# Block attention inside a matmul pipeline: scores of both float32 parts in two full-height passes instead of three half-height pairs

## The chip, the cores and the metric

One core of a Trainium2 chip runs the whole program. The metric is the device time of one execution in microseconds (us), as the median of several executions.

## The reference

Three layers follow each other. The attention layer has 4 batches, 8 heads, 768 tokens and 64 elements per head; each token sees the 4 first keys (the sinks) and the 127 keys before it and itself (the window):

```python
scores = scale * np.matmul(q, k.transpose(0, 1, 3, 2))
keep = is_sink | in_window
scores = np.where(keep, scores, -1000000000.0)
scores = scores - np.max(scores, axis=-1, keepdims=True)
a = np.exp(scores)
a = a / (np.sum(a, axis=-1, keepdims=True) + 1e-09)
out = np.matmul(a, v)
```

Its output, 3072 tokens of 512 elements, goes through a layer of 512 x 2048 x 512 with a squared ReLU (`w_in`, `w_out`), and then through a layer of 8 experts, of which each token uses the one with its highest gate score (`w1`, `w2`).

## The kernel before, in words

The tokens are worked in 12 blocks of 256, numbered t = 0 to 11. The matmul layer of block t runs on TensorE while the attention of block t + 1 is woven between its pieces. A block of the matmul layer has 16 steps j: `l1` (L610) does 12 matmuls of 256 columns into the tile psh, `l2` (L635) does 6 matmuls of 512 columns into the pair psx. The last stage, the experts, comes after all attention.

Float32 values are held as two parts of 'fp32r' type, hi and lo, of which hi is a rounded copy and lo the rest. A product is made of three matmuls, hi times hi, hi times lo and lo times hi, from block 2 on (T32 = 2; the first two blocks use plain float32).

The attention of a block handles four pairs p of heads and, for each, two halves n of 128 queries. The two heads e = 0, 1 of a pair lie on rows 0 to 63 and 64 to 127. Its pieces are:

- `prep_k` (L366): three (or two) 128x128 transposes of keys into a tile psk_ of the one bank psT; ScalarE copies it to the hi part of kT (L387), VectorE subtracts to get the lo part (L388).
- `prep_q` (L395): two transposes of queries into a tile of the bank s0 (L400); hi by ScalarE (L415), lo by VectorE (L416). GpSimd then splits the values V (L422, L423).
- `scores` (L446): per head one bank, s0 for head 0 and s1 for head 1 (psS, one buffer each). Three rounds m, in each a matmul for head 0 and one for head 1, each with 64 rows of contraction:

```python
for m, (a_, b_) in enumerate(((0, 0), (0, 1), (1, 0)) if t >= T32 else ()):
    for e in range(2):
        r = slice(64 * e, 64 * e + 64)
        PE.matmul(ps[e][:, 0:W], lhsT=qt[r, a_, n, :], rhs=kt[r, b_, c0:c0 + W], start=(m == 0), stop=(m == 2))
```

  W is 260 columns (4 of them the sinks), 128 for the first 128 queries of a batch. Then VectorE takes mask and row maximum of each head (L469), ScalarE the exponential (L472), and sums, reciprocals and scaling follow (L474 to L484). GpSimd collects sink weights in psk (L487 to L489).
- `ptrans` (L492): the probabilities are transposed into the bank psT (L501), split by ScalarE and VectorE (L512, L513) and masked by GpSimd (L517).
- `pv` (L523): matmuls with V into pso (L543), which ScalarE, VectorE and GpSimd add up (L548 to L553).
- `fin_sink` (L557) transposes psk into the bank psT, `add_sink` (L565) adds the share of the sinks.

Each piece is an event with a place h on a scale of two per step j (`attn_events`, L585); `run_to` emits the events up to a place between `l1` and `l2`. LEADS (L36) says how many units before its scores a key and a query preparation stand, and how many after them the transposes and the pv step. The instructions so emitted are ordered by a list scheduler by priority, within what data and buffers allow; `tc.high_priority` raises that of what is emitted inside it. Each engine then works its list in order.

Of the kernel before, what the change touches and what calls it, by code (L numbers as in the profile page):

```python
# [29 lines left out]
HOME = 224  # L30
REG = NT + 128
XW = 513
T32 = 2


LEADS = ((5, 2, 4.5, 8.5), (5, 2, 4.5, 8), (5.5, 2.5, 4.5, 8))  # L36

SPLITS = {6: (0, 0), 8: (2, 0), 11: (0, 1), 12: (1, 0), 13: (2, 1), 14: (3, 0)}

# [7 lines left out]
def kern(ctx, tc, q, k, v, n_sink, window, w_in, w_out, w_gate, w_og, w1, w2, out):  # L47
# [282 lines left out]


    nat = {}
    qTt = {}
    kTt = {}
    Vt = {}
# [30 lines left out]
    def prep_k(t, p):  # L366
        o = 1 if t % 3 == 0 else 0
        x = nat.pop(("k", t, p))
        ps = psT.tile([128, 4, 128], F32, tag="T", name="psk_")
        if t == 0:  # L370
            fill(ps[:].rearrange("p n c -> p (n c)"), 1)
        for n in range(o, 3):
            PE.transpose(ps[:, n], x[:, n].rearrange("p h d -> p (h d)"), ident[:])
        kt = att.tile([128, 2, KS * 3], F32R, tag="kT", name="kT", bufs=2)
        kv = kt[:].rearrange("p a (n c) -> p a n c", c=KS)
        if t < T32:
            kf = kv[:, 0].bitcast(F32)
# [9 lines left out]
        A.activation(out=kv[:, 0, o:3, 0:128], in_=ps[:, o:3], func=AF.Copy)  # L387
        V.tensor_tensor(out=kv[:, 1, o:3, 0:128], in0=ps[:, o:3], in1=kv[:, 0, o:3, 0:128].bitcast(F32), op=ALU.subtract)  # L388
        if o:
            G.tensor_copy(out=sk[:, p], in_=kv[:, :, 1, 0:NS].bitcast(F32))  # L390
        for n in range(o, 2):
            G.tensor_copy(out=kv[:, :, n, 128:KS], in_=sk[:, p].bitcast(F32))
        kTt[t, p] = kt

    def prep_q(t, p):  # L395
        x = nat.pop(("q", t, p))
        if t < T32:
            ps = psO.tile([128, 4, 128], F32, tag="O", name="psq")
        else:
            ps = psS.tile([128, 260], F32, tag="s0", name="psq")[:, 0:256].rearrange("p (n c) -> p n c", n=2)  # L400
# [4 lines left out]
        o = att.tile([128, 2, 2, 128], F32R, tag="qT", name="qT", bufs=2)  # L405
        qTt[t, p] = o
        if t < T32:
            if p % 2:
                A.activation(out=o[:, 0].bitcast(F32), in_=ps[:, 0:2], func=AF.Copy)
            else:  # L410
                V.tensor_copy(out=o[:, 0].bitcast(F32), in_=ps[:, 0:2])
            Vt[t, p] = nat.pop(("v", t, p))
            more(t, p)
            return
        A.activation(out=o[:, 0], in_=ps[:, 0:2], func=AF.Copy)  # L415
        V.tensor_tensor(out=o[:, 1], in0=ps[:, 0:2], in1=o[:, 0].bitcast(F32), op=ALU.subtract)  # L416

        n0 = 1 if t % 3 == 0 else 0
        x = nat.pop(("v", t, p))
# [26 lines left out]
    def scores(t, p, n):  # L446
# [6 lines left out]
        if t == 0 and n % 2:  # L453
            ps = [psX.tile([128, 512], F32, tag=f"x{e}", name=f"psx{e}") for e in range(2)]
        else:
            ps = [psS.tile([128, 260], F32, tag=f"s{e}", name=f"pss{e}") for e in range(2)]
        if t == 0:
            fill(ps[0][:, 0:W], 2)
        for e in range(2 if t < T32 else 0):
            r = slice(64 * e, 64 * e + 64)  # L460
            PE.matmul(ps[e][:, 0:W], lhsT=qt[r, 0, n, :].bitcast(F32), rhs=kt[r, 0, c0:c0 + W].bitcast(F32), start=True, stop=True)
# [93 lines left out]
    skT = {}  # L555

    def fin_sink(t):  # L557
        ps = psT.tile([128, 4, 128], F32, tag="T", name="psst")
# [26 lines left out]
    def attn_events(t):  # L585

        ev = []
        h0 = 32 * (t - 1) - 8
        a0, a1, a2, a3 = LEADS[min(t, 2)]
# [601 lines left out]
```

## Time and profile before

| what | value |
|---|---|
| median of 3 runs | 1150.24 us (1148.74 to 1150.37) |
| the profiled execution | 1149.1 us, its span 1147.4 us |
| PE busy | 1120.3 us (98%) |
| VectorE (DVE) busy | 728.4 us (63%) |
| ScalarE (ACT) busy | 638.2 us (56%) |
| GpSimd (POOL) busy | 419.8 us (37%) |

The span runs from the first to the last instruction; the execution's own time is 1.7 us longer. Shares of busy time are means over stages: attention of blocks 3 to 11 stands between about 178 and 720 us, the experts behind about 760 us. A matmul's time in the profile is that from its entry to its modelled end, and matmuls overlap; so what one costs is read from the starts of those that follow.

### The profile page before, as it was taken

What the parts mean: (1) busy time and instruction counts of PE and PEld (TensorE: products, weight loads), DVE (VectorE), ACT (ScalarE), POOL (GpSimd) and SP (SyncE); (2) the same over time, 40 slices, a digit from 0 to 9 for tenths busy, and PEclk for the clock granted to TensorE, in tenths of its full rate; (3) what the DMA queues carried; (4) which work ended last, traced back from release to release, by engine and by line L of the source; (5) the groups of instructions that cost most, each with busy time, mean ns of one, the idle gap of its engine ahead of it and who ended that gap; (6) DMA issues with size and microseconds to landing.
All of it is one profiled execution on the core that took longest, in us unless ns stands there. A gap on an engine that the chain in (4) does not pass through costs nothing. (4 is left out here: it accounts for less than half of the span.)

```text
span 1147.4 us, 23733 instructions
## 1 busy us (share of the span) xinstructions
PE 1120.3 (98%) x7002; PEld 939.0 (82%) x7002; DVE 728.4 (63%) x2027; ACT 638.2 (56%) x1749; POOL 419.8 (37%) x917
## 2 busy tenths in 40 slices
PE   7999999999999999999999999999999999999995
PEld 4556788888888888888888888997788888888884
DVE  4899876676767667676667677567312576764153
ACT  4898676777677767676767777464232232232200
POOL 3112553355664336565326665210211112221111
PEclk8999999999999999999999999999999999999998
DMA  6677111111211111211112110295411456653110
GB/s 150 172 238 208 44 25 50 40 50 38 54 29 50 38 45 38 56 29 43 36 38 56 38 31 2 42 242 159 129 39 47 156 185 216 225 203 133 48 45 24
DMA packets 139391, 100.08 MB, mean 87 GB/s; under 512 B 103907, under 2 KB 112227, under 8 KB 139238
## 3 DMA queue, kind: packets, MB, share of 16 engines
q1 hardware_dynamic: 131476, 82.28, 25.6%
q0 software_dynamic: 5472, 14.19, 3.7%
q10 hardware_dynamic: 2290, 1.84, 0.5%
q8 instruction: 64, 1.05, 0.4%
q14 instruction: 89, 0.73, 0.2%
HBM read 85.56 MB, written 13.76 MB: 87 GB/s over the span
## 5 line engine op out<-in xcount | busy, mean ns | idle before, releaser
L619 PE MATMUL psh<-xT,WI 128*128 128x256 f32 x2112 | 280.2, 282 | 0.0
L619 PEld LDWEIGHTS psh<-xT,WI 128*128 128x128 f32 x2112 | 266.5, 188 | 9.7 <-issue 0.5
L956 PE MATMUL psh<-WI,xt 128*128 (+1 forms) x672 | 163.7, 398 | 1.1 <-ACT xt L936 0.7
L629 DVE TENSOR_TENSOR r<-r 128x256 f32<-128x256 f32 x180 | 83.4, 464 | 113.2 <-ACT r L622 113.1
L644 PE MATMUL psx<-WOb,h 128*128 128x512 f32 x576 | 153.9, 404 | 0.8 <-ACT h L631 0.4
L956 PEld LDWEIGHTS psh<-WI,xt 128*128 128x128 f32 x672 | 125.0, 190 | 27.3 <-ACT xt L936 0.9
L644 PE MATMUL psx<-WOa,h 128*128 128x512 f32 x528 | 144.7, 409 | 0.0
L644 PEld LDWEIGHTS psx<-WOb,h 128*128 128x128 f32 x576 | 101.7, 188 | 20.0 <-ACT h L631 1.4
L472 ACT ACTIVATE P<-P,st 128x260 f32<-128x260 f32 (+1 forms) x192 | 93.7, 488 | 43.5 <-DVE st L469 43.1
L972 DVE TENSOR_TENSOR ht<-psht,ht 128x512 fp32r<-128x512 f32 x56 | 38.5, 689 | 120.8 <-ACT ht L936 120.4
L622 ACT ACTIVATE r<-psh 128x256 f32<-128x256 f32 x192 | 71.7, 373 | 63.0 <-PE psh L619 59.1
L644 PEld LDWEIGHTS psx<-WOa,h 128*128 128x128 f32 x528 | 93.4, 190 | 15.6
L517 POOL TENSOR_SCALAR_AFFINE_SELECT PT<-PT 128x256 fp32r<-128x256 f32 x224 | 98.5, 473 | 16.1 <-DVE PT L513 15.9
L994 POOL DMA_INDIRECT out_dram<-xg,pidx x28 | 28.7, 1025 | 199.9 <-ACT xg L993 159.2
L632 DVE TENSOR_TENSOR h<-r,h 128x256 fp32r<-128x256 f32 x184 | 83.7, 455 | 18.0 <-ACT h L631 12.2
L631 ACT ACTIVATE h<-r 128x256 fp32r<-128x256 f32 x184 | 76.1, 414 | 28.6 <-DVE r L629 23.8
L469 DVE CUSTOM_DVE_ANT_0 P<-pss,M 128x260 f32<-128x260 f32 (+1 forms) x184 | 72.6, 403 | 23.0 <-PE pss L465 11.1
L962 ACT ACTIVATE r<-psh 128x512 f32<-128x512 f32 x48 | 28.8, 599 | 100.2 <-PE psh L956 98.4
L985 PE MATMUL psy<-WOb,ht 128*128 (+1 forms) x336 | 84.0, 398 | 0.0
L985 PE MATMUL psy<-WOa,ht 128*128 (+1 forms) x336 | 82.2, 391 | 0.0
L484 ACT ACTIVATE P<-P,st 128x132 f32<-128x132 f32 (+2 forms) x168 | 62.2, 415 | 34.4 <-DVE st L475 34.3
L553 POOL TENSOR_TENSOR xr<-tB,tC 128x128 f32<-128x128 f32 x80 | 38.4, 480 | 101.8 <-DVE tB L552 96.7
(450 smaller groups left out, 1963.1 us busy)
## 6 DMA issues: line engine op xcount, KB each, us to landing
raw<-in_moe_w_dram SPq DMA_DIRECT2D x36, 1024.0 KB
craw<-in_moe_w_out_dram SPq DMA_DIRECT2D x15, 512.0 KB
craw<-in_moe_w_in_dram SPq DMA_DIRECT2D x14, 512.0 KB
x2tab<-x2s SPq DMA_DIRECT2D x24, 256.5 KB
kn<-in_k_dram SPq DMA_DIRECT2D x64, 96.0 KB
vn<-in_v_dram SPq DMA_DIRECT2D x64, 96.0 KB
qn<-in_q_dram SPq DMA_DIRECT2D x92, 64.0 KB
kn<-in_k_dram SPq DMA_DIRECT2D x32, 64.0 KB
```

The costliest lines, as they stand in the source:

```text
L469: V.tensor_tensor_reduce(out=P[:, e, 0:W], in0=ps[e][:, 0:W], in1=mask[:, 0:W], scale=-SCALE, scalar=3.0e38, op0=ALU.add, op1=ALU.min, acc ...
L472: A.activation(out=P[:, e, 0:W], in_=P[:, e, 0:W], func=AF.Exp, scale=-1.0, bias=st[:, e:e + 1], accum_out=st[:, 4 + e:5 + e])
L484: A.activation(out=P[:, e, 0:W], in_=P[:, e, 0:W], func=AF.Copy, scale=st[:, 6 + e:7 + e])
L517: G.affine_select(out=both[:, 1 - b, e], in_=bf[:, 0, e], pattern=[[0, 2], [1 - 2 * b, 128]], compare_op=ALU.is_gt if b else ALU.is_ge, fi ...
L619: PE.matmul(ps[:], lhsT=WI[:, j, a_, kk, :], rhs=x[:, b_, kk, :], start=(n == 0), stop=(n == 11))
L622: A.activation(out=hq[:], in_=ps[:], func=AF.Relu)
L629: E_.tensor_tensor(out=hq[:], in0=hq[:], in1=hq[:], op=ALU.mult)
L631: A.activation(out=o[:, 0], in_=hq[:], func=AF.Copy)
L632: V.tensor_tensor(out=o[:, 1], in0=hq[:], in1=o[:, 0].bitcast(F32), op=ALU.subtract)
L644: PE.matmul(acc[t][m][:], lhsT=o[:, a_, 128 * m:128 * m + 128], rhs=WO[j // 8][:, j % 8, b_, :], start=(j == 0 and n == 0), stop=(j == NF ...
L956: PE.matmul(ps[:], lhsT=o[:, a_, kk, :], rhs=wview(n, par + 2048 * b_ + 512 * kk, 512), start=(c == 0), stop=(c == 11))
L985: PE.matmul(yp[s][:], lhsT=o[:, a_, kk, :], rhs=wview(2 + n, par + 2048 * b_ + 512 * kk, 512), start=(n == 0 and kk == 0 and c == 0), stop ...
```

## The change

From block 3 on (STK = 3), five things change:

- `scores` does two matmuls per head with 128 rows of contraction. The keys of head e lie as 128 rows in kT[:, e]: the hi part on the head's own 64 rows, the lo part on the other 64. The first matmul has the queries' hi part on both halves, the second the lo part on the head's own rows and zeros on the others. The sum is the same three products.
- `prep_k` writes its transposes to the bank s0, and ScalarE and VectorE each take two instructions of 64 rows instead of one of 128.
- `prep_q` keeps one tile qst for all later blocks; ScalarE and VectorE take two instructions of 64 rows each, and GpSimd copies the hi parts to the other half. The zeros are written once.
- The row maxima of both heads are emitted at a priority raised by 100; a line of LEADS for t = 3 and later moves keys (5.5 to 6.5 units ahead), transposes (4.5 to 3.95 units behind) and pv (8 to 7.92).
- `fin_sink` uses the bank s1 and stands 0.91 units later.

The buffer of the query tile goes from two of half the size to one of the same total size; blocks 0 to 2 compute as before.

```diff
+T32, STK = 2, 3
+HALF = (slice(0, 64), slice(64, 128))
-LEADS = ((5, 2, 4.5, 8.5), (5, 2, 4.5, 8), (5.5, 2.5, 4.5, 8))
+LEADS = ((5, 2, 4.5, 8.5), (5, 2, 4.5, 8), (5.5, 2.5, 4.5, 8), (6.5, 2.5, 3.95, 7.92))
...
     def prep_k(t, p):
-        ps = psT.tile([128, 4, 128], F32, tag="T", name="psk_")
+        if t < STK:
+            ps = psT.tile([128, 4, 128], F32, tag="T", name="psk_")
+        else:
+            ps = psS.tile([128, 512], F32, tag="s0", name="psk_")[:].rearrange("p (n c) -> p n c", n=4)
...
+        else:
+            for e in range(2):
+                A.activation(out=kv[HALF[e], e, o:3, 0:128], in_=ps[HALF[e], o:3], func=AF.Copy)
+            for e in range(2):
+                V.tensor_tensor(out=kv[HALF[1 - e], e, o:3, 0:128], in0=ps[HALF[e], o:3], in1=kv[HALF[e], e, o:3, 0:128].bitcast(F32),
+                                op=ALU.subtract)
...
     def prep_q(t, p):
+            if "s" not in qbuf:
+                o = qbuf["s"] = att.tile([128, 2, 2, 2, 128], F32R, tag="qT", name="qst", bufs=1)
+                for e in range(2):
+                    r = HALF[1 - e]
+                    G.tensor_copy(out=o[r, 1, e].rearrange("p n (a c) -> p (n a) c", c=64),
+                                  in_=ident[r, None, 64 * e:64 * e + 64].broadcast_to([64, 4, 64]))
+            for e in range(2):
+                A.activation(out=o[HALF[e], 0, e], in_=ps[HALF[e], 0:2], func=AF.Copy)
+            for e in range(2):
+                V.tensor_tensor(out=o[HALF[e], 1, e], in0=ps[HALF[e], 0:2], in1=o[HALF[e], 0, e].bitcast(F32), op=ALU.subtract)
+            for e in range(2):
+                G.tensor_copy(out=o[HALF[1 - e], 0, e], in_=o[HALF[e], 0, e].bitcast(F32))
...
     def scores(t, p, n):
+        for e in range(2 if t >= STK else 0):
+            for a_ in range(2):
+                PE.matmul(ps[e][:, 0:W], lhsT=qt[:, a_, e, n, :], rhs=kt[:, e, c0:c0 + W], start=(a_ == 0), stop=(a_ == 1))
-        for m, (a_, b_) in enumerate(((0, 0), (0, 1), (1, 0)) if t >= T32 else ()):
+        for m, (a_, b_) in enumerate(((0, 0), (0, 1), (1, 0)) if T32 <= t < STK else ()):
...
-        for e in range(2):
-            V.tensor_tensor_reduce(out=P[:, e, 0:W], in0=ps[e][:, 0:W], in1=mask[:, 0:W], scale=-SCALE, scalar=3.0e38,
-                                   op0=ALU.add, op1=ALU.min, accum_out=st[:, e:e + 1])
+        with (tc.high_priority(100) if t >= STK else ExitStack()):
+            for e in range(2):
+                V.tensor_tensor_reduce(out=P[:, e, 0:W], in0=ps[e][:, 0:W], in1=mask[:, 0:W], scale=-SCALE, scalar=3.0e38,
+                                       op0=ALU.add, op1=ALU.min, accum_out=st[:, e:e + 1])
...
     def fin_sink(t):
+        else:
+            ps = psS.tile([128, 512], F32, tag="s1", name="psst")[:].rearrange("p (n c) -> p n c", n=4)
...
-            ev.append((h0 + 31, lambda: fin_sink(t)))
+            ev.append((h0 + (31 if t < STK else 31.91), lambda: fin_sink(t)))
```

Three places in the engines' lists show the moves. On PE, in block 4, around one `scores` call followed by a key preparation (psh and psx are `l1` and `l2`, pso the pv step, pspt the transposed probabilities, psk_ the keys), the order before is this; the two L465 rows stand there three times in turn:

```order
L543 MATMUL pso<-PT,V 128x256 x4
L465 MATMUL pss_4329<-kT,qT 128x260
L465 MATMUL pss_4330<-kT,qT 128x260
L501 MATMUL pspt<-ident,P 128x128 x2
L644 MATMUL psx_4005<-WOa,h_4189 128x512 x3
L644 MATMUL psx_4006<-WOa,h_4189 128x512 x3
L619 MATMUL psh<-xT,WI 128x256 x12
L373 MATMUL psk__4386<-ident,kn 128x128 x3
```

The same place of the changed kernel:

```order
L579 MATMUL pso<-PT,V 128x256 x4
L537 MATMUL pspt<-ident,P 128x128 x2
L496 MATMUL pss_4344<-kT,qst 128x260 x2
L496 MATMUL pss_4345<-kT,qst 128x260 x2
L683 MATMUL psx_4006<-WOa,h_4193 128x512 x3
L683 MATMUL psx_4007<-WOa,h_4193 128x512 x3
L378 MATMUL psk__4370<-ident,kn 128x128 x3
L658 MATMUL psh<-xT,WI 128x256 x12
```

Six half-height score matmuls became four of full height, the transposes of the probabilities stand ahead of the scores, and the key transposes stand one `l1` earlier, right behind the first `l2`.

On VectorE, the rows from the first row maximum of a `scores` call to the query part that follows, before (the row that reads out the accumulator behind each maximum is left out):

```order
L469 ISA P,st<-pss_4709,M_137 128x260
L632 TENSOR_TENSOR h_4693<-r,h_4693 128x256
L551 TENSOR_TENSOR tB<-pso,tB 64x128
L552 TENSOR_TENSOR tB<-pso,tB 64x128
L469 ISA P,st<-pss_4710,M_137 128x260
L513 TENSOR_TENSOR PT<-pspt,PT 128x2x128
L474 TENSOR_SCALAR st<-st 128x2
L416 TENSOR_TENSOR qT<-psq,qT 128x256
```

And in the changed kernel:

```order
L505 ISA P,st<-pss_4725,M_137 128x260
L505 ISA P,st<-pss_4726,M_137 128x260
L671 TENSOR_TENSOR h_4699<-r,h_4699 128x256
L587 TENSOR_TENSOR tB<-pso,tB 64x128
L588 TENSOR_TENSOR tB<-pso,tB 64x128
L549 TENSOR_TENSOR PT<-pspt,PT 128x2x128
L510 TENSOR_SCALAR st<-st 128x2
L446 TENSOR_TENSOR qst<-psq,qst 64x256 x2
```

The second maximum moved ahead of three other operations, and the query part is two instructions of 64 rows.

On GpSimd, the rows of the same call between the pv sum and the sink weights, before:

```order
L553 TENSOR_TENSOR xr<-tB,tC 128x128
L517 AFFINE_SELECT PT<-PT 128x256 x4
L487 CAST psk_142<-P 128x2x4
L488 CAST psk_142<-P 128x2x4
L489 TENSOR_TENSOR psk_142<-P,psk_142 128x2x4
```

And in the changed kernel:

```order
L589 TENSOR_TENSOR xr<-tB,tC 128x128
L553 AFFINE_SELECT PT<-PT 128x256 x4
L448 CAST qst<-qst 64x256 x2
L523 CAST psk_142<-P 128x2x4
L524 CAST psk_142<-P 128x2x4
L525 TENSOR_TENSOR psk_142<-P,psk_142 128x2x4
```

The two copies of the queries' hi part stand behind the four masks and ahead of the sink weights.

## Rows read from the trace of the kernel before

**Rows 1.** The page, part 1: busy time, share of the span, instructions of each engine.
```profile
PE 1120.3 (98%) x7002; PEld 939.0 (82%) x7002; DVE 728.4 (63%) x2027; ACT 638.2 (56%) x1749; POOL 419.8 (37%) x917
```

**Rows 2.** Busy time by stretch: from:to, length, busy time of PE, PEld, DVE, ACT, POOL, clock, DMA.
```profile
298.80:359.20 60.40, 60.40 (x446) 53.80 (x445) 43.22 (x152) 43.08 (x132) 37.01 (x90) 1.00 0.15 38
800.00:1147.40 347.40, 333.96 (x1618) 276.21 (x1616) 163.34 (x175) 79.27 (x138) 65.94 (x56) 0.98 0.36 120
```

**Rows 3.** Waits of PE, 178 to 720 us: total us, times, longest; the first of four.
```profile
PE psc L754 <- DVE x2U L679: 0.4, 1, 0.4
```

**Rows 4.** Timeline of PE around one scores call: start, us to the last's end, instruction, count.
```profile
302.63 0.49 PE L373 MATMUL psk__4662<-ident,kn 128*128 128x128 f32 x3
302.88 1.64 PE L644 MATMUL psx<-WOb,h 128*128 128x512 f32 x6
304.35 1.57 PE L619 MATMUL psh<-xT,WI 128*128 128x256 f32 x12
305.76 0.64 PE L543 MATMUL pso<-PT,V 128*128 128x256 f32 x4
306.32 0.63 PE L465 MATMUL pss<-kT,qT 64*128 64x260 f32 x6
306.88 0.44 PE L501 MATMUL pspt<-ident,P 128*128 128x128 f32 x2
307.08 1.62 PE L644 MATMUL psx<-WOb,h 128*128 128x512 f32 x6
308.54 0.38 PE L404 MATMUL psq<-ident,qn 128*128 128x128 f32 x2
308.68 0.60 PE L619 MATMUL psh<-xT,WI 128*128 128x256 f32 x3
```

**Rows 5.** The same call in a shorter window: its first four matmuls.
```profile
306.32 0.51 PE L465 MATMUL pss<-kT,qT 64*128 64x260 f32 x4
```

**Rows 6.** Timeline of PE around a scores call with 128 columns.
```profile
177.50 0.64 PE L543 MATMUL pso<-PT,V 128*128 128x256 f32 x4
178.07 0.55 PE L465 MATMUL pss<-kT,qT 64*128 64x128 f32 x6
178.75 1.63 PE L644 MATMUL psx<-WOb,h 128*128 128x512 f32 x6
```

**Rows 7.** Timeline of PE: other matmuls with 64 rows, once a batch.
```profile
236.32 0.43 PE L438 MATMUL psv<-vshl,sel 64*128 64x64 f32 x2
236.68 1.68 PE L619 MATMUL psh<-xT,WI 128*128 128x256 f32 x12
```

**Rows 8.** Groups by line and shape, PE, 178 to 720 us: count, busy us, mean ns.
```profile
L465 PE MATMUL pss<-kT,qT 64*128 64x260 f32 x360 | 37.6, 314 | 0.0
L465 PE MATMUL pss<-kT,qT 64*128 64x128 f32 x72 | 6.6, 289 | 0.0
```

**Rows 9.** Timeline of the other engines around the same scores call as rows 4.
```profile
303.08 0.70 ACT L484 ACTIVATE P<-P,st 128x132 f32<-128x132 f32 x2 [0.70 <-DVE st L475]
307.09 0.43 DVE L469 CUSTOM_DVE_ANT_0 P<-pss,M 128x260 f32<-128x260 f32 x1 [0.29 <-POOL V L422]
309.52 1.75 POOL L517 TENSOR_SCALAR_AFFINE_SELECT PT<-PT 128x256 fp32r<-128x256 f32 x4 [0.24 <-DVE PT L513]
313.86 0.62 PE L465 MATMUL pss<-kT,qT 64*128 64x260 f32 x6
```

**Rows 10.** Groups by line and shape, 178 to 720 us: key and query parts, a cast.
```profile
L387 ACT ACTIVATE kT<-psk__4662 128x384 fp32r<-128x384 f32 x1 | 0.5, 479 | 0.0
L388 DVE TENSOR_TENSOR kT<-psk__4662,kT 128x384 fp32r<-128x384 f32 x1 | 0.6, 558 | 0.0
L415 ACT ACTIVATE qT<-psq 128x256 fp32r<-128x256 f32 x35 | 12.7, 364 | 0.0
L416 DVE TENSOR_TENSOR qT<-psq,qT 128x256 fp32r<-128x256 f32 x35 | 14.1, 404 | 0.0
L422 POOL CAST V<-vn 128x192 fp32r<-128x192 f32 x48 | 20.4, 450 | 55.4 <-PE pso L543 55.4
```

More of the change, by code (lines that the diff above doesn't have):

```diff
@@ L32 @@
 XW = 513
-T32 = 2
-LEADS = ((5, 2, 4.5, 8.5), (5, 2, 4.5, 8), (5.5, 2.5, 4.5, 8))
+T32, STK = 2, 3
+HALF = (slice(0, 64), slice(64, 128))
+LEADS = ((5, 2, 4.5, 8.5), (5, 2, 4.5, 8), (5.5, 2.5, 4.5, 8), (6.5, 2.5, 3.95, 7.92))
 SPLITS = {6: (0, 0), 8: (2, 0), 11: (0, 1), 12: (1, 0), 13: (2, 1), 14: (3, 0)}
@@ L332, in kern @@
     nat = {}
+    qbuf = {}
     qTt = {}
@@ L386, in prep_k @@
             return
-        A.activation(out=kv[:, 0, o:3, 0:128], in_=ps[:, o:3], func=AF.Copy)
-        V.tensor_tensor(out=kv[:, 1, o:3, 0:128], in0=ps[:, o:3], in1=kv[:, 0, o:3, 0:128].bitcast(F32), op=ALU.subtract)
+        if t < STK:
+            A.activation(out=kv[:, 0, o:3, 0:128], in_=ps[:, o:3], func=AF.Copy)
+            V.tensor_tensor(out=kv[:, 1, o:3, 0:128], in0=ps[:, o:3], in1=kv[:, 0, o:3, 0:128].bitcast(F32), op=ALU.subtract)
+        else:
[4 more added lines that the diff above has]
+                                op=ALU.subtract)
         if o:
@@ L399, in prep_q @@
         else:
-            ps = psS.tile([128, 260], F32, tag="s0", name="psq")[:, 0:256].rearrange("p (n c) -> p n c", n=2)
+            ps = psS.tile([128, 512], F32, tag="s0", name="psq")[:, 0:256].rearrange("p (n c) -> p n c", n=2)
         if t == 0:
@@ L404, in prep_q @@
             PE.transpose(ps[:, n], x[:, n].rearrange("p h d -> p (h d)"), ident[:])
-        o = att.tile([128, 2, 2, 128], F32R, tag="qT", name="qT", bufs=2)
-        qTt[t, p] = o
+        if t < STK:
+            own = t // T32
+            if own not in qbuf:
+                qbuf[own] = att.tile([128, 2, 2, 2, 128], F32R if own else F32, tag="qT", name=f"qT{own}", bufs=1)
+            o = qbuf[own][:, p % 2]
+            qTt[t, p] = o
         if t < T32:
             if p % 2:
-                A.activation(out=o[:, 0].bitcast(F32), in_=ps[:, 0:2], func=AF.Copy)
+                A.activation(out=o[:, 0], in_=ps[:, 0:2], func=AF.Copy)
             else:
-                V.tensor_copy(out=o[:, 0].bitcast(F32), in_=ps[:, 0:2])
+                V.tensor_copy(out=o[:, 0], in_=ps[:, 0:2])
             Vt[t, p] = nat.pop(("v", t, p))
@@ L414, in prep_q @@
             return
-        A.activation(out=o[:, 0], in_=ps[:, 0:2], func=AF.Copy)
-        V.tensor_tensor(out=o[:, 1], in0=ps[:, 0:2], in1=o[:, 0].bitcast(F32), op=ALU.subtract)
+        if t < STK:
+            A.activation(out=o[:, 0], in_=ps[:, 0:2], func=AF.Copy)
+            V.tensor_tensor(out=o[:, 1], in0=ps[:, 0:2], in1=o[:, 0].bitcast(F32), op=ALU.subtract)
+        else:
[5 more added lines that the diff above has]
+                                  in_=ident[r, None, 64 * e:64 * e + 64].broadcast_to([64, 4, 64]))
+            o = qbuf["s"]
+            qTt[t, p] = o
+            for e in range(2):
[4 more added lines that the diff above has]
+                G.tensor_copy(out=o[HALF[1 - e], 0, e], in_=o[HALF[e], 0, e].bitcast(F32))
         n0 = 1 if t % 3 == 0 else 0
@@ L455, in scores @@
         else:
-            ps = [psS.tile([128, 260], F32, tag=f"s{e}", name=f"pss{e}") for e in range(2)]
+            ps = [psS.tile([128, 512], F32, tag=f"s{e}", name=f"pss{e}") for e in range(2)]
         if t == 0:
@@ L460, in scores @@
             r = slice(64 * e, 64 * e + 64)
-            PE.matmul(ps[e][:, 0:W], lhsT=qt[r, 0, n, :].bitcast(F32), rhs=kt[r, 0, c0:c0 + W].bitcast(F32), start=True, stop=True)
-        for m, (a_, b_) in enumerate(((0, 0), (0, 1), (1, 0)) if t >= T32 else ()):
+            PE.matmul(ps[e][:, 0:W], lhsT=qt[r, 0, n, :], rhs=kt[r, 0, c0:c0 + W].bitcast(F32), start=True, stop=True)
+        for e in range(2 if t >= STK else 0):
+            for a_ in range(2):
+                PE.matmul(ps[e][:, 0:W], lhsT=qt[:, a_, e, n, :], rhs=kt[:, e, c0:c0 + W], start=(a_ == 0), stop=(a_ == 1))
+        for m, (a_, b_) in enumerate(((0, 0), (0, 1), (1, 0)) if T32 <= t < STK else ()):
             for e in range(2):
@@ L557, in fin_sink @@
     def fin_sink(t):
-        ps = psT.tile([128, 4, 128], F32, tag="T", name="psst")
+        if t < STK:
+            ps = psT.tile([128, 4, 128], F32, tag="T", name="psst")
+        else:
+            ps = psS.tile([128, 512], F32, tag="s1", name="psst")[:].rearrange("p (n c) -> p n c", n=4)
         for n in range(2):
@@ L588, in attn_events @@
         h0 = 32 * (t - 1) - 8
-        a0, a1, a2, a3 = LEADS[min(t, 2)]
+        a0, a1, a2, a3 = LEADS[min(t, 3)]
         for p in range(4):
```

## The prediction

> **What bounds the kernel now.** I read the page's busy times first, then the stretches, then the waits of PE, then PE's timeline around single calls. PE is busy for 98% of the span, the next engine for 63% [rows 1]. In the stretch of block 5's attention PE is busy for 60.40 of 60.40 us, with VectorE at 43.2, ScalarE at 43.1 and GpSimd at 37.0 us of the same 60.4 [rows 2]. From 178 to 720 us PE waits four times for another engine, 1.0 us in all, the longest 0.4 us [rows 3]. So between these two places the time is PE's own work, and what counts is how far apart its instructions start. Behind that the experts keep PE busy for 334 of 347 us [rows 2]; they begin when attention has let go of its memory, so an earlier end of attention moves them as a whole.
>
> **What a scores call costs on PE.** Starts are read from [rows 4]. Twelve full-height matmuls of 256 columns take 1.41 us (304.35 to 305.76), 0.1175 each, 0.46 ns per column. Four pv matmuls of the same size then take 0.56 where four times 0.1175 is 0.47: 0.09 is lost between the last of them and the first score matmul. The six half-height score matmuls take 0.56. Two transposes behind them take 0.20, where the two query transposes take 0.14 (308.54 to 308.68): 0.06 more. Inside the call the two heads do run side by side: the fourth matmul ends 0.51 after the first one's start [rows 5], the sixth 0.63 [rows 4], so a pair costs 0.12, what one full-height matmul of 260 columns costs at 0.46 ns per column. Three pairs would be 0.36; the rest, about 0.20, and the 0.09 and 0.06 around the call are paid for going into and out of half height. That it goes with the shape and not with the scores is seen at another place: two matmuls with 64 rows and only 64 columns hold PE for 0.36 us (236.32 to 236.68) [rows 7].
>
> The Trainium skill ("TensorEngine Tiling (Array Packing)", Key Properties) says that changing the tiling mode drains TensorE. The trace agrees with 0.09 us at the entry and 0.06 at the exit.
>
> **The sum for PE.** Changed, the stretch from the first pv matmul to the `l2` behind is four pv matmuls (0.47), two transposes (0.14) and four full-height matmuls of 260 columns (4 x 0.1195 = 0.48): 1.09 us. Before it is 305.76 to 307.08, 1.32 us. That gives 0.23 per call; with starts rounded to 10 ns I take 0.225. The slower first matmul behind a transpose is paid once in both orders. There are 360 such matmuls in blocks 3 to 11, at six a call 60 calls [rows 8]: 13.5 us. The other 12 calls (72 matmuls) have 128 columns [rows 8]. Before, one stretch is 177.50 to 178.75, 1.25 us [rows 6]. No row has a full-height matmul of 128 columns and this type; by columns alone it is 0.06, by the third key transpose (0.25 for three, 0.14 for two [rows 4]) 0.11, by the 256-column matmul 0.1175. I take 0.11, since the transpose also has 128 columns and a weight load for each: 1.25 - (0.47 + 0.14 + 0.44) = 0.20, for 12 calls 2.4 us, with ends of 2.0 and 4.9. In sum PE has 15.9 us less to do.
>
> **What is added elsewhere, and what covers it.** Half-row instructions have as many columns as the full ones, so I price each like the whole (the lower end is half). Per pair ScalarE gets one more of 0.48 and one of 0.36, VectorE one of 0.56 and one of 0.40, GpSimd two copies that I put at the 0.45 of a cast [rows 10]. With four pairs a block that is 3.4, 3.8 and 3.6 us, or 46.5, 47.0 and 40.6 of the 58.6 us that a block would take: 79, 80 and 69%. PE's own work hides this as long as no single chain comes late. Three can.
>
> - The bank s0. The query transposes start 2.22 us after the first score matmul, and the maximum of head 0, which frees the bank, ends at 307.52, 1.20 after it [rows 4, 9]: 1.0 us to spare. In the changed order key or query transposes come 0.48 + 1.46, about 1.95 us after; but head 0 is complete after two matmuls rather than five, about 0.2 earlier, and its maximum stands first. That leaves 0.75 to 0.95, enough for one more VectorE operation in front. It holds now for 36 key preparations as well as 36 query ones. No cost.
> - The probabilities. They are ready at 303.78 and transposed at 306.88 [rows 4, 9]: 3.1 us to spare. The transposes now stand ahead of the scores (0.56 + 0.14 earlier), the period is 0.23 shorter, and up to 0.96 of key copies may run ahead on ScalarE: 1.2 us are left. No cost.
> - The queries' copies on GpSimd. The masks end at 311.27, the next scores start at 313.86 [rows 9]; two copies of 0.45 end at 312.2, some 1.5 us ahead of them. Behind the copies is the sink weights' work, which the sink transposes wait for, and these now share the bank s1 with head 1, which they hold until ScalarE has copied them (0.36, like [rows 10] for the same shape, plus what runs in front). Between them and head 1's matmuls PE has 0.47 + 0.14 + 0.24 us. I take 0.15 lost in each of six blocks, 0.9 us, between 0 and 0.3 each.
>
> The single query tile costs nothing: the scores that read it stand ahead of the next transposes on PE. SP's queue only has query loads a place or two earlier. The first use in block 3 has two more copies; I take 0.6, between 0 and 1.5.
>
> The sum: 1149.1 of the profiled execution (span 1147.4) - 15.9 + 1.5 = 1134.7. The median of the runs, 1150.24, lies 1.1 higher, and so I forecast **1135.8** on that scale.
>
> **The rivals.**
>
> *The fourth pass is paid and nothing comes back.* The 0.20 inside a call, the 0.09 and the 0.06 might not belong to half height but to scores as such, for instance to operands that are just finished. Then three slots of 0.12 become four: 60 x 0.12 + 12 x 0.11 = 8.5 us more, 1158.7. For it speaks that pairs run at full overlap [rows 4, 5]; against it are the other 64-row matmuls [rows 7]. The Trainium skill ("TensorEngine Tiling (Array Packing)", Theoretical Speedup) gives up to twice the speed for a contraction of 64 or less, and so by this rule alone the change would lose. The trace agrees with that rule inside the call only. Chance 0.04.
>
> *The bank s0 becomes the wait.* It decides once head 0's maximum ends later than 1.95 us after the call's first matmul; from 2.17 on the wait eats the whole gain at each of 72 preparations. If VectorE, at 80%, had two operations in front of it (0.97 more), the miss would be up to 0.2 for each, near 14 us: the result would be about 1150. With three (1.4 more) it would be 0.6 at each, 43 us, some 1178. Against it: the maximum is ranked first. Chance 0.04 for slower, 0.03 for no change.
>
> *Half of it is given back.* VectorE and ScalarE at 80% come late now and then, with probabilities or the parts of `l1`'s output; 0.1 us a call is 7 us, 1142.8. For it speaks how little is idle on three engines at once; against it the spare times above. Chance 0.12.
>
> **How the numbers follow.** The forecast, with PE's waits anywhere from none to 4 us more than the sum has, gets 0.77. Its own range comes from the ends: 4.9 instead of 2.4 for short calls, and no waits, is 1131.8; 2.0 for them, the two waits at their upper ends (1.8 and 1.5) and 2 us of others is 1140. The half case reaches beyond; the range 1131.5 to 1142.5 holds 0.8 or a little more. About 0.2% (2.3 us) is what a measurement of this kernel can tell from no change. Faster by more than that: 0.77 + 0.12 = 0.89, and 0.02 from smaller misses at the bank, 0.91. Same: 0.03. Slower: 0.06, the rest of the first two rivals.
>
> **What would show it.** Right: the stretch from the first pv matmul to the `l2` behind the scores takes 1.09 us, blocks are 58.5 to 58.8 us long rather than 60.4, PE's waits from 178 us on stay under 3 us, the experts begin about 15 us earlier and are as long as before. Wrong: gaps of 0.09 us still around the four matmuls; PE waiting at the key or query transposes for VectorE's maximum, at the probabilities' transposes for ScalarE, or at the scores for GpSimd's copies.

## The result and the profile after

The changed kernel takes 1138.49 us (median of 6 runs, 1136.49 to 1141.55), the one before 1148.56 us in the same session (6 runs, 1147.93 to 1150.37): a ratio of 0.990 with a 95% interval of 0.9887 to 0.9913, 10.1 us less. The profiled execution took 1136.49 us, its span is 1134.6 us; that of before was 1149.1 and 1147.4. The forecast was 1135.8, the range 1131.5 to 1142.5. In a later session the changed kernel took 1135.84 us beside 1146.56 (0.9908, 0.9893 to 0.9923).

The page's busy times of the changed kernel, to hold against [rows 1]:

```profile
PE 1103.5 (97%) x6858; PEld 939.1 (83%) x6858; DVE 775.5 (68%) x2099; ACT 667.1 (59%) x1821; POOL 438.6 (39%) x991
```

PE has 144 matmuls less (72 calls with two less each) and 16.8 us less busy time; VectorE (DVE) has 47 us more, ScalarE (ACT) 29, GpSimd (POOL) 19. The same two stretches as in [rows 2], one block of attention and the experts (from:to, length, busy time of PE, PEld, DVE, ACT, POOL, clock, DMA):

```profile
295.50:354.30 58.80, 58.80 (x429) 54.08 (x428) 48.39 (x158) 46.24 (x140) 39.01 (x98) 1.00 0.16 38
787.25:1134.60 347.35, 333.94 (x1624) 276.34 (x1622) 164.44 (x181) 79.66 (x138) 66.88 (x56) 0.99 0.36 120
```

A block takes 58.8 us instead of 60.4, and PE is still busy through all of it. The granted clock is 1.00 in both kernels' blocks, so nothing in them is the clock's. The two stretches of the experts are windows of one length up to the end of the span; where the experts begin is read from their first transposes, before and changed:

```profile
780.86 0.38 PE L942 MATMUL psxt<-ident,xg 128*128 128x128 f32 x2
769.62 0.38 PE L981 MATMUL psxt<-ident,xg 128*128 128x128 f32 x2
```

They begin 11.2 us earlier, and from there to the end it is 366.5 us before and 365.0 changed; the 1.5 us between are taken up under the scale below. PE's waits from 178 to 720 us, as the list of waits has them (it leaves out the short ones), to hold against [rows 3]:

```profile
PE psv L470 <- DVE pf L734: 0.9, 3, 0.3
PE psq L416 <- DVE st L505: 0.6, 1, 0.6
PE psc L793 <- DVE x2U L718: 0.4, 1, 0.4
```

PE's timeline around a scores call that corresponds to the one of [rows 4] (start, us to the last's end, instruction, count):

```profile
302.91 0.63 PE L579 MATMUL pso<-PT,V 128*128 128x256 f32 x4
303.38 0.38 PE L537 MATMUL pspt<-ident,P 128*128 128x128 f32 x2
303.51 0.73 PE L496 MATMUL pss<-kT,qst 128*128 128x260 f32 x4
304.07 1.53 PE L683 MATMUL psx<-WOb,h 128*128 128x512 f32 x6
305.44 0.38 PE L416 MATMUL psq<-ident,qn 128*128 128x128 f32 x2
```

From the first pv matmul to the query transposes it is 2.53 us, where [rows 4] have 2.78. The 0.09 behind the pv matmuls is gone (four take 0.47), the transposes take 0.13 rather than 0.20, and four full-height score matmuls take 0.56. Of that 0.56, 0.085 is the slower first matmul behind a transpose, which before was paid by the first `l2` matmul (six took 1.46, now 1.37). So the stretch from the first pv matmul to the `l2` is 1.16 us here and not the 1.09 of the prediction, and the difference comes back inside the `l2`. By the medians of all starts between the beginnings of blocks 2 and 11 the gain of a call is 0.228 us: 0.091 behind pv, 0.081 in the scores, 0.056 at the transposes.

A call of 128 columns, to hold against [rows 6]:

```profile
177.95 0.64 PE L579 MATMUL pso<-PT,V 128*128 128x256 f32 x4
178.43 0.56 PE L496 MATMUL pss<-kT,qst 128*128 128x128 f32 x4
178.82 0.41 PE L537 MATMUL pspt<-ident,P 128*128 128x128 f32 x2
178.99 0.47 PE L683 MATMUL psx<-WOb,h 128*128 128x512 f32 x1
```

It is 1.04 us where before it is 1.25; its transposes still stand behind the scores in both. Nine calls of 128 columns in the new order gain 0.19 each by the medians of the starts, the `l2` or `l1` behind included. VectorE at the call of 260 columns above, to hold against the DVE row of [rows 9]:

```profile
304.15 0.43 DVE L505 CUSTOM_DVE_ANT_0 P<-pss,M 128x260 f32<-128x260 f32 x1 [0.20 <-POOL V L454]
304.50 0.08 DVE L505 DVE_READ_ACCUMULATOR2_ANT st<- 128x1 f32 x1
```

Head 0's maximum starts 0.64 us after the first score matmul and ends at 304.58; the next transposes into the bank s0 start at 305.44, 0.86 later. The prediction had 0.75 to 0.95 to spare.

### The profile page after: what moved, and what is told of

Read it like the earlier page. It is cut to its first block, busy times and chain, and to the rows that moved or that the text cites. A ratio compares the mean times of both kernels' runs of the same rounds, so it can differ in the third digit from the quotient of the medians.

```text
span 1134.6 us, 23905 instructions
## 1 busy us (share of the span) xinstructions
PE 1103.5 (97%) x6858; PEld 939.1 (83%) x6858; DVE 775.5 (68%) x2099; ACT 667.1 (59%) x1821; POOL 438.6 (39%) x991
## 5 line engine op out<-in xcount | busy, mean ns | idle before, releaser
L658 PE MATMUL psh<-xT,WI 128*128 128x256 f32 x2112 | 283.6, 283 | 0.0
L683 PE MATMUL psx<-WOb,h 128*128 128x512 f32 x576 | 150.5, 398 | 1.4 <-ACT h L670 1.1
L683 PE MATMUL psx<-WOa,h 128*128 128x512 f32 x528 | 138.8, 398 | 0.0
L668 DVE TENSOR_TENSOR r<-r 128x256 f32<-128x256 f32 x180 | 90.3, 502 | 59.2 <-ACT r L661 57.9
L670 ACT ACTIVATE h<-r 128x256 fp32r<-128x256 f32 x184 | 76.4, 415 | 58.8 <-DVE r L668 56.1
L966 POOL DMA_INDIRECT xg<-x2tab,pidx x30 | 41.0, 1366 | 92.7 <-issue 59.5
L505 DVE CUSTOM_DVE_ANT_0 P<-pss,M 128x260 f32<-128x260 f32 (+1 forms) x184 | 68.1, 397 | 12.4 <-PE pss L500 3.7
```

The source lines that it names most:

```text
L658: PE.matmul(ps[:], lhsT=WI[:, j, a_, kk, :], rhs=x[:, b_, kk, :], start=(n == 0), stop=(n == 11))
L668: E_.tensor_tensor(out=hq[:], in0=hq[:], in1=hq[:], op=ALU.mult)
L670: A.activation(out=o[:, 0], in_=hq[:], func=AF.Copy)
L683: PE.matmul(acc[t][m][:], lhsT=o[:, a_, 128 * m:128 * m + 128], rhs=WO[j // 8][:, j % 8, b_, :], start=(j == 0 and n == 0), stop=(j == NF ...
L966: G.indirect_dma_start(out=x, out_offset=None, in_=x2tab[:] if s >= PRE else x2tab[0:256 * (NBLK - 3)], in_offset=bass.IndirectOffsetOnAxi ...
```

## The experiments

Twelve runs, in three sessions with a median of the kernel before of 1146.58, 1147.22 and 1146.56 us. Theory and rival are those of the prediction: T says that a pair of half-height matmuls costs one slot of 0.12 us and that going in and out of half height costs some 0.35 once a call; the rivals say that the scores' cost has another cause, or that a bank becomes the wait. "Changed" is the changed kernel. Where a sum over a stretch is given, it is that of PE's starts from the beginning of block 2 to that of block 11, where 69 of the 72 calls of blocks 3 to 11 are worked: 540.36 us before, 528.03 changed.

### Everything moved, scores as before

```diff
-        for e in range(2 if t >= STK else 0):
-            for a_ in range(2):
-                PE.matmul(ps[e][:, 0:W], lhsT=qt[:, a_, e, n, :], ...)
-        for m, (a_, b_) in enumerate(((0, 0), (0, 1), (1, 0)) if T32 <= t < STK else ()):
+        for m, (a_, b_) in enumerate(((0, 0), (0, 1), (1, 0)) if t >= T32 else ()):
```

The operands are those of the kernel before, too.

> Everything that the change moves (key transposes in bank s0, sink transposes in bank s1, row maxima ranked up, places of the events), but the scores stay six half-height matmuls with the operands of before. Theory (the gain is the way into and out of half height that is no longer taken): the call keeps its 0.56 us and most of the 0.09 and 0.06 around it, so the stretch from the first pv matmul to the l2 behind takes 1.2 to 1.35 us and the time stays within 5 us of the kernel before, 1143 to 1150. Rival (the gain comes from order, banks and ranks): 1137 to 1141, as the changed kernel.

Measured: 1162.99 us, 1.0148 of before (1.0131 to 1.0165), slower than both kernels and than both expectations. PE's timeline around a call, and the longest wait:

```profile
306.43 0.63 PE L576 MATMUL pso<-PT,V 128*128 128x256 f32 x4
306.90 0.38 PE L534 MATMUL pspt<-ident,P 128*128 128x128 f32 x2
307.21 0.63 PE L497 MATMUL pss<-kT,qT 64*128 64x260 f32 x6
307.77 1.66 PE L680 MATMUL psx<-WOb,h 128*128 128x512 f32 x6
```

```profile
PE psk__8907 L378 <- DVE st L502: 1.0, 1, 1.0
```

The stretch from the first pv matmul to the `l2` is 1.34 us, as T has it. The loss at the entry has gone with the scores: it now stands behind the transposes (306.90 to 307.21, 0.31 instead of 0.13), and the scores take 0.56 as ever. By all starts a call costs 0.27 us more than changed. It is thus the half height that costs, whatever stands beside it, and nothing here shows a gain from the moves alone. The rest of the loss are waits of the key transposes for the maximum that frees s0 (8 of them, 5.3 us): with the six matmuls head 0 is complete one round later, and VectorE has taken up another operation. The bank s0, a rival of the prediction, decides here.

### The stacking alone

```diff
-        with (tc.high_priority(100) if t >= STK else ExitStack()):
+        with ExitStack():
-        a0, a1, a2, a3 = LEADS[min(t, 3)]
+        a0, a1, a2, a3 = LEADS[min(t, 2)]
-            ps = psS.tile([128, 512], F32, tag="s0", name="psk_")...
+            ps = psT.tile([128, 4, 128], F32, tag="T", name="psk_")
```

The sink transposes go back to psT as well.

> Only the stacked operands and the four full-height matmuls; banks, ranks and places as before. Theory: the call costs 4 x 0.12 = 0.48 us, nothing is lost around it, and PE has the same 15 us less to do; the time is 1134 to 1141, with waits of PE that may differ from those of the changed kernel by a few us. Rival (order, banks and ranks bring the gain): 1146 to 1150, or slower, since ScalarE, VectorE and GpSimd have more to do.

Measured: 1169.59 us, 1.0202 (1.0185 to 1.0219). PE's own work fell as T says: the score matmuls stand 0.12 apart with nothing lost ahead of them, and the scores' share of the stretch is 32.80 us (37.72 before). But PE waits 20.7 us by the list of waits, almost all at the bank psT. The two longest of the list by total and by single wait, then VectorE and PE at one key preparation:

```profile
PE psg L702 <- DVE PT L546: 5.0, 6, 0.8
PE psk__10165 L375 <- DVE PT L546: 1.0, 1, 1.0
```

```profile
304.34 0.29 DVE L507 TENSOR_SCALAR st<-st 128x2 f32<-128x2 f32 x1 [0.37 <-ACT P L505]
305.06 0.42 DVE L546 TENSOR_TENSOR PT<-pspt,PT 128x256 fp32r<-128x256 f32 x1
305.54 0.55 PE L375 MATMUL psk__4666<-ident,kn 128*128 128x128 f32 x3
```

The split of the probabilities (L546), which frees psT, now stands on VectorE's list behind a step that itself waits 0.37 us for an exponential (L507). The keys get the bank at 305.48. It stands so in all 20 of the listed waits of key and gate transposes, while before nearly every such split (67 of 71) stands right behind head 1's maximum. The work of PE was as T has it and the time some 30 us beyond it, past the rival's figure too, in the main because VectorE's list has another order; by the starts some 29 us more than before stand ahead of the tiles in psT.

### The second pass at half height

```diff
-            for a_ in range(2):
-                PE.matmul(ps[e][:, 0:W], lhsT=qt[:, a_, e, n, :], rhs=kt[:, e, c0:c0 + W], ...)
+            PE.matmul(ps[e][:, 0:W], lhsT=qt[:, 0, e, n, :], rhs=kt[:, e, c0:c0 + W], ...)
+        for e in range(2 if t >= STK else 0):
+            PE.matmul(ps[e][:, 0:W], lhsT=qt[HALF[e], 1, e, n, :], rhs=kt[HALF[e], e, c0:c0 + W], ...)
```

> The changed kernel with its second pass at half height: the low part of the queries times the high part of the keys with 64 rows, the two heads in turn; the zeros are not used. Theory: three slots of 0.12 us, but the way in and out of half height is paid again, about 0.1 each, so a call costs 0.5 to 0.65 where it costs 0.48 now, and the time is 1139 to 1150. Rival (the rule that two matmuls of 64 rows share the array, with nothing paid for the switch): a call costs 0.36, 72 x 0.12 = 8.6 us less than the changed kernel, 1128 to 1131.

Measured: 1151.07 us, 1.0045 (1.0029 to 1.0062), a little above T's range and 20 us from the rival's.

```profile
305.99 0.49 PE L495 MATMUL pss<-kT,qst 128*128 128x260 f32 x2
306.41 0.38 PE L497 MATMUL pss<-kT,qst 64*128 64x260 f32 x2
306.72 1.67 PE L684 MATMUL psx<-WOb,h 128*128 128x512 f32 x6
308.22 0.38 PE L416 MATMUL psq<-ident,qn 128*128 128x128 f32 x2
```

The four score matmuls take 0.73 us rather than 0.56, and the `l2` behind them 1.50 rather than 1.37: 0.27 more a call by the medians of the starts (0.168 and 0.104), although a pair of 0.12 stands in place of two matmuls of 0.12. So the two changes of height cost 0.12 + 0.27 = 0.39 us here. That is T in kind, with the switch a little dearer than the 0.35 around the call of before and about twice what the expectation had put on it (some 0.1 each way). PE waits for nothing else (0.6 us listed), and the stretch is 16.0 us longer than changed.

### A third full-height pass

```diff
-            for a_ in range(2):
+            for a_ in (0, 1, 2):
-                PE.matmul(... lhsT=qt[:, a_, e, n, :], ... stop=(a_ == 1))
+                PE.matmul(... lhsT=qt[:, min(a_, 1), e, n, :], ... stop=(a_ == 2))
```

> The changed kernel with a third full-height matmul per head (the low part of the queries is counted twice). Theory (PE is the bound and a pass costs its columns): 60 x 2 x 0.1195 + 12 x 2 x 0.11 = 17.0 us more than the changed kernel, 1152 to 1158. Rival (PE is no longer the bound in these blocks, the other engines at 80% are): less than 8 us more.

Measured: 1153.09 us, 1.0062 (1.0045 to 1.0079), in T's range. The six matmuls of a call:

```profile
305.88 0.97 PE L496 MATMUL pss<-kT,qst 128*128 128x260 f32 x6
306.69 1.55 PE L683 MATMUL psx<-WOb,h 128*128 128x512 f32 x6
```

They take 0.81 us where four take 0.56: 0.123 for each more, 0.111 for one of 128 columns. The scores' share grows by 16.2 us, the stretch by 14.5. PE is the bound, and nearly all that is added to it shows in the end.

### One head after the other, at half height

```diff
-        for m, (a_, b_) in enumerate(((0, 0), (0, 1), (1, 0)) if t >= T32 else ()):
-            for e in range(2):
+        for e in range(2 if t >= T32 else 0):
+            for m, (a_, b_) in enumerate(((0, 0), (0, 1), (1, 0))):
```

> The kernel before, with the three half-height matmuls of head 0 first and then the three of head 1, so that no two neighbours lie on different rows. Theory (a pair of two heads shares its 0.12 us, so three pairs cost about 0.36 us inside plus some 0.35 us for going into and out of half height): a pair falls apart into two matmuls, 0.36 us more for each of 60 calls of 260 columns and about 0.2 for 12 of 128, so 20 to 26 us more than before: 1167 to 1176 us, and the six matmuls of a call about 0.9 us from the first start to the instruction behind. Rival (the two heads do not run side by side, the pairs only look so by modelled ends): no difference, 1145 to 1150 us.

Measured in one execution: 1155.44 us, 8 more than the median of before, neither of the two.

```profile
187.72 0.63 PE L465 MATMUL pss<-kT,qT 64*128 64x260 f32 x6
188.28 0.44 PE L501 MATMUL pspt<-ident,P 128*128 128x128 f32 x2
```

The call takes the same 0.56 us. The trace shows why the expectation of 20 to 26 failed: of the six matmuls, those that signal the end of a head are third and sixth in the program, but they are the fifth and sixth to start, 6 ns apart (188.068 and 188.074). In all 76 calls that the trace has with their six matmuls the two signals are the fifth and sixth. Head 1's first matmul has therefore not waited for head 0's other two; the rows 0 to 63 and 64 to 127 work off their own matmuls side by side, whatever the order in the program. The Trainium skill ("TensorEngine Tiling (Array Packing)", Key Properties) says that tiles operate independently and can execute in parallel; this trace agrees. The 8 us are waits in the same stretch (6.0 us more), of the key transposes (1.7) and the gate's transposes (2.7) above all; no start in a call differs by more than 0.01 us.

### A fourth half-height round

```diff
-        for m, (a_, b_) in enumerate(((0, 0), (0, 1), (1, 0)) if t >= T32 else ()):
+        for m, (a_, b_) in enumerate(((0, 0), (0, 1), (1, 0), (1, 1)) if t >= T32 else ()):
```

> The kernel before with a fourth round of half-height matmuls, low part of the queries times low part of the keys (a term that the reference's sum does not need). It gives the price of one more pair by itself, with no other going in or out of half height. Theory (a pair costs about 0.12 us and going in and out some 0.35 us once for a call): 60 times 0.12 and 12 times about 0.06, 7 to 9 us more than before, 1154 to 1157 us; the run with one head after the other asks only for a change of the words, any two neighbours share a slot. Rival (six half-height matmuls are six slots of 0.12 us with nothing for the switch, which gives the same 0.72 us for a call): 60 times 0.24 and 12 times 0.12, 15 to 17 us more, 1162 to 1165 us.

Measured in one execution: 1185.16 us, 38.6 more than before; both theories were far off in the time. The call itself, and the wait at the bank:

```profile
201.23 0.74 PE L465 MATMUL pss<-kT,qT 64*128 64x260 f32 x8
201.90 0.44 PE L501 MATMUL pspt<-ident,P 128*128 128x128 f32 x2
```

```profile
PE psq L404 <- DVE st L469: 8.4, 24, 0.4
```

Head 0's maximum of this call on VectorE, 2.15 us behind the first score matmul where [rows 9] have 0.77:

```profile
203.38 0.43 DVE L469 CUSTOM_DVE_ANT_0 P<-pss,M 128x260 f32<-128x260 f32 x1
```

Eight matmuls take 0.67 where six take 0.56: by the medians 0.118 for the pair more (0.112 at 128 columns), and the scores' share of the stretch is 8.2 us larger. That is T's 7 to 9, and half of the rival's; so a pair is one slot, and the 0.35 is paid once a call. The rest came from VectorE: its list here has an `h` split and two sums of pv between the `l1` square and head 0's maximum, and every one of 34 query transposes stands about 0.3 us or more behind its place (15.4 us in all); key transposes add 4.9.

### Which of the accompanying moves the gain needs

Three runs undo one move each, with the rest as changed. The bank and place of the sink transposes and the single query tile were not undone alone.

```diff
-        with (tc.high_priority(100) if t >= STK else ExitStack()):
+        with ExitStack():
```

> The changed kernel without the raised priority of the row maxima; everything else as changed. Theory (the stacking collects its gain only where the bank s0 is free for the next key or query transposes, and the priority does that): VectorE takes the maxima behind other operations of 0.5 us, PE waits at psk_ and psq for VectorE's maximum at some of the 72 preparations, 0.2 to 0.6 us each, 1142 to 1156 us. Rival (0.75 to 0.95 us of slack at s0 is enough for one or two operations in front, so the priority does nothing): within 2 us of the changed kernel, 1136 to 1141 us, waits of PE from 178 to 720 us under 4 us.

Measured: 1155.87 us, 1.0075 (1.0056 to 1.0094), at the upper end of the theory.

```profile
391.91 0.42 DVE L671 TENSOR_TENSOR h<-r,h 128x256 fp32r<-128x256 f32 x1
392.37 0.69 DVE L557 TENSOR_TENSOR PT<-pspt,PT 128x512 fp32r<-128x512 f32 x1
392.97 0.28 DVE L505 CUSTOM_DVE_ANT_0 P<-pss,M 128x128 f32<-128x128 f32 x1
393.32 0.44 PE L378 MATMUL psk__6078<-ident,kn 128*128 128x128 f32 x2 [1.63 <-DVE st L505]
```

Without the rank the maximum stands behind a square, two sums, a split of `h` and one of the probabilities, and the keys wait 1.63 us. The list of waits has 14 at key transposes, 13.6 us, of which six are 1.6 or more.

```diff
-        if t < STK:
-            ps = psT.tile([128, 4, 128], F32, tag="T", name="psk_")
-        else:
-            ps = psS.tile([128, 512], F32, tag="s0", name="psk_")...
+        ps = psT.tile([128, 4, 128], F32, tag="T", name="psk_")
```

> The changed kernel with the key transposes in the bank psT again, as before; places and priority stay as changed. Theory (of the accompanying moves it is the key's bank that counts: the key transposes wait in psT for VectorE's split of the probabilities, as in the run with the stacking alone): waits of 0.5 to 1.0 us at psk_ at 15 to 36 preparations, 1146 to 1165 us. Rival (the waits of that run came from the old places or ranks, and with the new ones psT is free in time): 1136 to 1142 us.

Measured: 1162.93 us, 1.0131 (1.0109 to 1.0152), the theory.

```profile
399.25 0.69 DVE L554 TENSOR_TENSOR PT<-pspt,PT 128x512 fp32r<-128x512 f32 x1
400.02 0.20 PEld L375 LDWEIGHTS psk__6078<-ident,kn 128*128 128x128 f32 x2 [1.00 <-issue]
400.05 0.41 PE L375 MATMUL psk__6078<-ident,kn 128*128 128x128 f32 x2 [0.82 <-issue]
```

The profile names "issue", but the transposes start 0.1 us after the split of the probabilities that frees psT (399.94): a bank, as in the run with the stacking alone. There are 27 such waits, 16.2 us, and each of them ends 0.1 us behind such a split.

```diff
-        a0, a1, a2, a3 = LEADS[min(t, 3)]
+        a0, a1, a2, a3 = LEADS[min(t, 2)]
```

> The changed kernel with the places of before for keys (5.5), probability transposes (4.5) and pv (8); banks and priority stay as changed. Theory (the places only decide how long the operands have, and the banks and the priority collect the gain): probability transposes stand behind the scores again, 0.14 us of work moves, a few waits of 0.2 to 0.5 us for the bank s0 come in, 1138 to 1146 us. Rival (the places are what keeps the banks from being waited for): PE waits at psk_, psq or pspt at most calls, 1150 us or more.

Measured: 1158.20 us, 1.0091 (1.0072 to 1.0111), the rival's time.

```profile
290.27 0.56 DVE L399 TENSOR_TENSOR kT<-psk__4389,kT 64x384 fp32r<-64x384 f32 x1
290.98 0.72 PE L496 MATMUL pss<-kT,qst 128*128 128x260 f32 x4 [0.48 <-DVE kT L399]
```

The scores wait for the keys themselves: the second of the two half-row subtracts, which the stacking brings, ends at 290.83. This wait is listed 18 times, 6.4 us, the one for the sink weights' copy 5 times, 3.4 us, and the gate's transposes wait 6 times, 3.0 us, for the split of the probabilities in psT. Keys that are made in twice as many instructions need the longer lead. So what the rival named (waits at the keys', queries' and probabilities' tiles) is not what happened, but its time is.

### Two versions that might have been faster

The changed kernel once more, in the session of these two:

> The changed kernel once more, for a time beside the two versions behind it. Every theory: 0.987 to 0.992 of before, 1134 to 1139 us.

Measured: 1135.84 us, 0.9908 (0.9893 to 0.9923).

The first version has two moves, from block 3 on:

```diff
     def prep_sink(b):
-        ps = psT.tile([128, 4, 128], F32, tag="T", name="psv")
+        ps = psS.tile([128, 512], F32, tag="s1", name="psv")...
     def fin_sink(t):
-        A.activation(out=o[:], in_=ps[:, 0:2], func=AF.Copy)
+        with tc.high_priority(100):
+            V.tensor_copy(out=o[:], in_=ps[:, 0:2])
```

> The changed kernel, with the copy of the transposed sink weights on VectorE at a raised priority instead of ScalarE, and the spread of the sink values in the bank s1 instead of psT (blocks 3 and later). Theory (the copy on ScalarE that stands behind a gate exponential holds head 1's scores 0.16 to 0.24 us in five blocks, about 1.0 us, and the spread waits 0.35 us three times for the bank psT): 1 to 2 us less than the changed kernel, 1133 to 1137 us, no wait of PE at psv and gaps of head 1's matmuls behind the sink transposes near 0.12 us. Rival (VectorE is fuller than ScalarE, so the copy is late there too, or a neighbour is pushed): no difference within 1 us, or up to 2 us slower.

Measured: 1136.94 us, 0.9919 (0.9905 to 0.9932): no gain.

```profile
295.86 0.42 DVE L609 CAST pskT<-psst 128x256 fp32r<-128x256 f32 x1
296.33 0.50 PE L500 MATMUL pss<-kT,qst 128*128 128x260 f32 x2 [0.46 <-DVE pskT L609]
```

The waits at psv went away, but on VectorE the copy stands behind the gate's small steps and holds head 1's scores 0.46 us, longer than on ScalarE; and the key transposes wait for s0 in three blocks. The move of the spread alone was not run.

```diff
-T32, STK = 2, 3
+T32, STK = 2, 2
```

> The same as the version with the two sink moves, and the new form of scores from block 2 on instead of block 3. Theory (block 2's eight calls stand in block 1's matmul stretch, where PE is the bound for most of the time, and each saves 0.23 to 0.25 us): 1.5 to 2 us less than without, 1131 to 1135 us. Rival (in block 1's stretch PE waits for the masks of the probabilities and for the sink transposes, together some 4 us, so the end of that stretch is set by another chain, or the new places suit a stretch that begins late badly): no gain, or slower by up to 2 us.

Measured, with both moves above and the new places for block 2 too: 1139.16 us, 0.9933 (0.9919 to 0.9946), 2.2 more than without. Block 1's stretch, where these scores stand, lasts 69.3 us instead of 67.9: there PE waits 2.2 us for the masks (1.5 without) and 1.0 us for GpSimd's first copy of queries. Neither version beats the changed kernel.

## Why the prediction was right, step by step

**PE is the bound.** Right: a block stays 100% PE, and a pass added to the scores costs its matmuls almost in full.

**The cost of a scores call.** Right in size and in kind. The forecast had 0.225 us for a call of 260 columns and 0.20 for one of 128; measured are 0.228 and 0.19, 60 x 0.228 + 12 x 0.19 = 16.0 us against the 15.9 of the sum. The sign of 1.09 us up to the `l2` is met as it was written where the order is that of before, in the run with the stacking alone (1.09 by the medians), and reads 1.16 in the changed order. A pair costs one slot (0.118, fourth round), a full-height matmul the same (0.123, third pass), and the change of height costs about 0.35 around six matmuls and 0.39 around two. The step that three of four slots were paid back by the switch is thus shown; the rival that the fourth pass is paid and nothing comes back, which would have lost 8.5 us, falls. The Trainium skill ("TensorEngine Tiling (Array Packing)", Theoretical Speedup) gives up to twice the speed for a dimension of 64 or less. The trace agrees for the pairs, 0.118 us for two matmuls, and not for the call: the change of height, 0.35 us, costs as much as three pairs save.

**What hides the added work.** Right for the other engines' shares (VectorE, ScalarE and GpSimd are busy for 82, 79 and 66% of a block where 80, 79 and 69 stood), and for the slack at s0: 0.86 us where 0.75 to 0.95 stood. What was not said is how it is kept. Each of the three moves that were undone alone costs 1.7 to 2.3% against changed (1.0075, 1.0091 and 1.0131 of before, beside 0.9908), and so costs the gain and about as much again.

**The waits.** This is the term that was mis-sized. The forecast had 1.5 us. The 69 calls of the stretch are 15.4 us of work less, and it became 12.33 us shorter (11.69 in the profile of the later session), so PE waits 3 to 4 us more than before in it; and the experts begin 11.2 us earlier (11.9 in the later profile) where about 15 stood, so by then it is 4 to 5 us. The list of waits shows little of this, since most are short. The sink transposes in s1 were foreseen at 0.9:

```profile
295.62 0.20 ACT L750 ACTIVATE gs<-gs 128x2 f32<-128x2 f32 x1 [0.89 <-DVE gs L748]
296.00 0.38 ACT L601 ACTIVATE pskT<-psst 128x256 fp32r<-128x256 f32 x1
296.42 0.30 PEld L496 LDWEIGHTS pss<-kT,qst 128*128 128x128 f32 x2 [0.17 <-ACT pskT L601]
```

ScalarE's copy (L601) stands behind a gate exponential that had waited 0.89 us; head 1's matmuls lose 0.15 to 0.24 in five of six blocks, 1.0 us together. Not foreseen was the spread of the sink values, three times (here at 411 us):

```profile
411.64 0.43 PE L470 MATMUL psv<-vshl,sel 64*128 64x64 f32 x2 [0.31 <-DVE pf L734]
413.19 0.68 DVE L472 TENSOR_TENSOR vsk<-psv,blkm 128x512 fp32r<-128x512 f32 x1
414.03 0.52 PE L537 MATMUL pspt<-ident,P 128*128 128x128 f32 x3
```

Its matmuls wait for VectorE to let go of the gate logits in psT, 1.1 us more than before in all by the starts, and then hold psT until 413.87, so that the transposes behind come 0.28 late here, 0.1 to 0.28 in the three. The first use of the new query tile, for which 0.6 stood, shows no wait in the list. Once in 72 times the bank s0 is late by 0.6 (the row psq above). Before had waits of its own, about 1.2 us at key transposes in psT, which are gone. The rest are short waits whose cause stays open. What was missed is thus in the sentence that three chains can come late: it followed the chains at the scores, and not the tiles that share psT and come once in three blocks.

**The scale.** From span to span the change is 12.8 us, by the medians 10.1 and 10.7. In the profile of before the granted clock stands at 1.2 GHz, half of its upper level, for 3.4 us in the experts; in the 10 us ahead of that PE was busy for 8.47.

```profile
814.75:818.15 3.40, 3.40 (x10) 2.66 (x9) 2.76 (x2) 0.00 (x0) 1.95 (x1) 0.50 0.66 251
```

The changed kernel's profile has nothing of the kind there. Counted from the experts' first transposes, the matmuls of both profiles start alike up to 794 us of before, and from 826 us on those of before are 1.5 us later. That much of the 12.8 us is the clock's and not the change's. Besides, the profiled execution of before lay above the medians of later sessions (1149.1 against 1146.6 to 1148.6), that of the change below its first one (1136.49 against 1138.49), and the forecast was scaled by a median of 1150.24 from three runs.

**The rivals.** Half of the gain was not given back: the waits took 4 to 5 of the 16.0 us. The bank s0 holds PE up in three of the versions: with six matmuls and the moves, without the rank, with a fourth round. In the changed kernel it is late once in 72 times; its 0.07 rested on that kernel's own list, and the slack belongs to that list alone.

## What to carry to other kernels

Where PE is busy throughout, price a matmul by the starts of what follows, and price a change between half and full height as an item of its own: a group at half height had to save more than about three slots of 0.12 us here before it pays. The saving on PE was only collected where the list of the engine that frees the banks was moved with it; read that list after every edit, since a list scheduler may put a step that waits ahead of the one that frees. Undo the accompanying moves one at a time before calling them harmless.

## What the runs showed of the hardware that was not expected

- The two row halves of PE take their matmuls independently of the program's order: three for one half and then three for the other take the same 0.56 us as in alternation (one execution).
- Half the columns saved little: one more full-height score matmul costs 0.123 us with 260 columns and 0.111 with 128, one more pair 0.118 and 0.112.
- An excursion into half height costs 0.35 to 0.39 us whether two, six or eight matmuls are inside.
